# A last layer of 2304 tokens: its first product by a seven-product scheme in three blocks of 768 tokens

## The chip, the cores and the metric

The kernel runs on one core of a Trainium2 chip. The metric is the device time of one execution in microseconds (us); the time before is the median of three runs. The trace is of one profiled execution. Engines: PE is TensorE, ACT is ScalarE, DVE is VectorE, POOL is GpSimd, SP issues the transfers.

## What is computed

The reference chains three layers: linear attention, a top-2 mixture of eight experts, and a last dense layer over all 2304 tokens of 512 features. The change concerns the last layer, and the gather that feeds it:

```python
out[mask] += top2_w[mask, k, None] * (h @ w2[e])   # experts, two per token
...
h = np.maximum(x @ w_in, 0.0)                      # 2304x512 @ 512x2048
return (h * h @ w_out).astype(np.float32)          # 2304x2048 @ 2048x512
```

## The kernel before

**Order.** The scheduling is manual: each engine runs its instructions in the order in which the Python code emits them, and semaphores join the engines. So the loops of the code are the order of the work. SP issues transfers in order too, and so does POOL with its gathers.

**Exact products from split numbers.** Every fp32 matrix is split in two fp32r parts, `hi` (a rounded copy, by ACT) and `lo` (the rest, a subtraction). A product takes three matmuls: hi·hi, hi·lo, lo·hi (`mm`, L97). Weights are loaded in pieces of 128x512 (`w_load`, L131) and split by ACT and POOL (`w_conv`, L136).

**Experts.** Ten parts (`for pt in range(1, NP)`, L1161), each of eight steps `f`. A step has the first product of its tokens (`e_1`) and the second one of the step before (`e_2`, L240). The last part, 9, has 352 tokens of expert 7. Each expert writes its rows to `y_d` in DRAM. Beside parts 2 to 8 the last layer's weights are widened into `win_d` and `wout_d`.

**Last layer.** Tokens come in 18 tiles of 128. `l_gather` (L1022) issues two indirect transfers on POOL for a tile, the rows `ya` and `yb` of its two experts; `l_sum` (L1038) weighs and adds them on ACT and DVE; `l_t` (L1044) transposes on PE and splits. There are five blocks, four of 512 tokens and one of 256. In a block, for each of 16 slices of 128 hidden features, `l_1` (L1057) makes 12 matmuls into a PSUM bank M0 or M1, ACT takes the relu and the rounded square, DVE the exact square and the low part; `l_2` (L1076) adds the slice's second product to one accumulator per token tile, one slice later:

```python
for u in range(NU + 1):
    m, f = divmod(u, NF2)
    if u < NU:
        l_1(u)
    if u > 0:
        l_2(u - 1)
```

The weights of the layer stay split in SBUF for all blocks; half of their pieces are loaded and split in parts 8 and 9, half in block 0. The four tiles of block 0 are gathered in part 9. They may read only rows of `y_d` that earlier parts have written (`YA_ROWS`); the router (`r_4`, L694) adds to a count when this would not do, and a slow path (L1222) then recomputes everything.

Of the kernel before, what the change touches and what calls it, by code (L numbers as in the profile page):

```python
# [32 lines left out]
def kernel(  # L33
# [25 lines left out]
    NTILE = B * R + B // 2  # L59
    DC = DM // 128  # L60
# [48 lines left out]
    runs = consts.tile([128, E], FT)  # L109

# [145 lines left out]
    with ExitStack() as actx:  # L256
# [437 lines left out]
        def r_4(g):  # L694
# [4 lines left out]
            yield  # L699
            nc.vector.tensor_add(runs, t[:, 1, 0], runs)  # L700
# [32 lines left out]
        def r_6(g):  # L733
# [211 lines left out]
    nc.vector.tensor_reduce(cf, runs, axis=AX.X, op=OP.max)  # L945
    nc.vector.tensor_copy(ci, cf)
# [7 lines left out]
    with ExitStack() as ectx:  # L954
# [63 lines left out]
        blocks = [[T0[b] + r for r in range(R)] for b in range(B)]  # L1018
        blocks.insert(1, [T0[b] + R for b in (1, 3)])
        X2, H2, OP_, YA = {}, {}, {}, {}  # L1020

        def l_gather(m, i):  # L1022
            t = blocks[m][i]
            if m == 0:
                if i == 0:
                    YA[-1] = ep.tile([128, R, DM], FT, name="ya0", tag="xg", bufs=1)
                ya = YA[-1][:, i]
                yb = ep.tile([128, DM], FT, name="yb", tag="wide", bufs=3)
            else:
                ya = ep.tile([128, DM], FT, name="ya", tag="ya", bufs=3)  # L1030
                yb = ep.tile([128, DM], FT, name="yb", tag="wide", bufs=3)
# [12 lines left out]
        def l_t(m, i):  # L1044
            ya, _ = YA.pop((m, i))
            if i == 0:
                X2[m] = [ep.tile([128, DC, 512], FR, name="x2", tag=x, bufs=1)
                         for x in (("xth", "xtl") if m % 2 == 0 else ("xg", "wd"))]
            t = bank("Tk" if m else ("Tk", "N0", "KV", "M0")[i], [128, DC, 128])
            for d in range(DC):  # L1050
                nc.tensor.transpose(t[:, d], ya[:, d * 128:d * 128 + 128], ident)  # L1051
            c = slice(i * 128, i * 128 + 128)
            hi_lo(X2[m][0][:, :, c], X2[m][1][:, :, c], t)

        NF2 = F2 // 128

        def l_1(u):  # L1057
            m, f = divmod(u, NF2)
            n = 128 * len(blocks[m])
            wh, wl = wt[2 * E + f // 4, 0]  # L1060
            fc = (f % 4) * 128
            xh, xl = X2[m]
            t = bank(f"M{u % 2}", [128, 512])
            for d in range(DC):
                for i, (a, b) in enumerate(((wh, xh), (wh, xl), (wl, xh))):
                    mm(t[:, :n], a[:, d, fc:fc + 128], b[:, d, :n], d == 0 and i == 0, d == DC - 1 and i == 2)
            r = ep.tile([128, 512], FT, name="r", tag="y", bufs=4)
            nc.scalar.activation(r[:, :n], t[:, :n], AF.Relu)  # L1068
            hh = ep.tile([128, 512], FR, name="h2h", tag="hh", bufs=2)
            hl = ep.tile([128, 512], FR, name="h2l", tag="hl", bufs=2)  # L1070
            nc.scalar.activation(hh[:, :n], r[:, :n], AF.Square)  # L1071
            nc.vector.tensor_mul(r[:, :n], t[:, :n], r[:, :n])  # L1072
            nc.vector.tensor_sub(hl[:, :n], r[:, :n], hh[:, :n].bitcast(FT))  # L1073
            H2[u] = (hh, hl)

        def l_2(u):  # L1076
            m, f = divmod(u, NF2)
            wh, wl = wt[2 * E + f // 4, 1]
            hh, hl = H2.pop(u)
            last = f == NF2 - 1  # L1080
            for j, tt in enumerate(blocks[m]):
                if f == 0:
                    OP_[j] = bank(ACC[j], [128, DM])
                c = slice(j * 128, j * 128 + 128)
                for i, (a, b) in enumerate(((hh, wh), (hh, wl), (hl, wh))):
                    mm(OP_[j], a[:, c], b[:, f % 4], f == 0 and i == 0, last and i == 2)
# [25 lines left out]
        for f in range(NF2 // 2):  # L1112
            pieces[NP, f], ahead = ahead[:2], ahead[2:]
# [212 lines left out]
```

## Time and profile before

| | us |
|---|---|
| median of 3 runs (lowest, highest) | 1069.35 (1068.01, 1069.85) |
| the profiled execution's own time | 1067.83 |
| its span in the trace | 1066.0 |
| PE busy | 1038.9 (97%) |
| DVE, ACT, POOL busy | 595.0, 471.1, 396.7 |

The span is what the trace covers; the execution's own time is 1.8 us longer. Busy time of matmuls is of overlapping instructions, so the rate of a stretch is better read from the chain of waits, which gives the start and the length of runs of instructions.

### The profile page before, as it was taken

Reading aid. Unit: us, or ns where it says so; the run is one execution under the profiler, and the core shown is the slowest. Engines: PE = TensorE matmul, PEld = TensorE weight load, DVE = VectorE, ACT = ScalarE, POOL = GpSimd, SP = SyncE. Lnnn points to the kernel's source line nnn. Section 1 sums busy time; section 2 is a strip of 40 time slices with the busy share of each in tenths; the row PEclk is TensorE's granted clock in tenths of the full one; section 3 lists DMA queues with packets and bytes.
Section 4 is the critical chain, followed back from the end, with each engine's and each line's share of the span. In section 5 each row is a group of like instructions: output and inputs, shape, how many; then the busy total and the mean of one; then the engine's idle time right before and its main releaser. Section 6 shows DMA issues by size and latency. Waiting matters only on the chain.

```text
span 1066.0 us, 18597 instructions
## 1 busy us (share of the span) xinstructions
PE 1038.9 (97%) x7132; PEld 874.8 (82%) x7132; DVE 595.0 (56%) x1192; ACT 471.1 (44%) x967; POOL 396.7 (37%) x374
## 2 busy tenths in 40 slices
PE   6999999899999999999999999999999999999997
PEld 4777677888888898998888888888988888888886
DVE  5778798812777777777778743432442332333222
ACT  4887777335354444535353544432332222222221
POOL 3444656645546454645545455540110010000000
PEclk9999999999999999999999999999999999999999
DMA  5976633465646465565656554320220011001001
GB/s 149 280 213 212 191 115 121 149 199 188 203 156 201 163 196 192 196 204 167 205 183 208 161 174 130 114 79 5 65 70 13 28 40 40 21 0 40 1 1 42
DMA packets 104048, 136.27 MB, mean 128 GB/s; under 512 B 17554, under 2 KB 58642, under 8 KB 103954
## 3 DMA queue, kind: packets, MB, share of 16 engines
q1 hardware_dynamic: 98194, 116.14, 34.8%
q0 software_dynamic: 5760, 18.88, 5.4%
q8 instruction: 58, 0.95, 0.4%
q14 instruction: 36, 0.29, 0.1%
HBM read 92.45 MB, written 42.54 MB: 127 GB/s over the span
## 4 chain that ended last, share of the span: by engine, by line
PE 90%; DVE 6%; ACT 2%; DMA 1%; issue 1%; POOL 0%; SPq 0%; ACTq 0%
PE M L98 38%; PE N L98 15%; PE KV L98 12%; PE Tq L98 8%; PE P L98 8%; PE kpair L98 2%; PE qpair L98 1%; DVE kd L428 1%; DVE kmx L426 1%; PE Tk L393 1%; PE M L200 1%; PE Tk L98 1%; PE Tk L1051 1%; PE Tk L200 1%; PE Tk L403 1%; DVE ps L513 1%
## 5 line engine op out<-in xcount | busy, mean ns | idle before, releaser
L1072 DVE TENSOR_TENSOR r<-M,r 128x512 f32<-128x512 f32 (+1 forms) x80 | 51.0, 638 | 248.3 <-ACT h2h L1071 248.3
L1068 ACT ACTIVATE r<-M 128x512 f32<-128x512 f32 (+1 forms) x80 | 44.5, 556 | 250.7 <-PE M L98 250.7
L229 ACT ACTIVATE hh<-M 128x304 fp32r<-128x304 f32 (+2 forms) x128 | 49.0, 422 | 210.6 <-PE M L98 210.3
L226 DVE SCALAR_TENSOR_TENSOR hl<-M,hh 128x304 fp32r<-128x304 f32 (+2 forms) x128 | 56.2, 470 | 109.1 <-ACT hh L229 109.0
L508 POOL PARTITION_ALL_REDUCE qmx<-ps x36 | 69.9, 1944 | 79.6 <-ACT ps L506 67.2
L1033 POOL DMA_INDIRECT ya<-y_d,yrows x18 | 17.9, 997 | 189.3 <-PE Tk L1051 113.6
L1073 DVE TENSOR_TENSOR h2l<-r,h2h 128x512 fp32r<-128x512 f32 (+1 forms) x80 | 57.7, 722 | 7.0
L1071 ACT ACTIVATE h2h<-r 128x512 fp32r<-128x512 f32 (+1 forms) x80 | 47.1, 589 | 2.5
L98 PE MATMUL M<-x,w30h 128*128 128x512 f32 (+1 forms) x160 | 46.1, 373 | 0.0
L98 PE MATMUL M<-x,w10h 128*128 128x512 f32 (+1 forms) x160 | 45.9, 372 | 0.0
L98 PE MATMUL M<-x,w20h 128*128 128x512 f32 (+1 forms) x160 | 45.8, 371 | 0.0
L98 PE MATMUL M<-x,w00h 128*128 128x512 f32 (+1 forms) x160 | 45.6, 369 | 0.0
L145 POOL TENSOR_TENSOR w30l<-wstage,w30h 128x512 fp32r<-128x512 f32 x20 | 27.7, 1386 | 46.7 <-ACT w30h L144 46.6
L98 PE MATMUL N<-kvc,qp 128*64 128x81 f32 x1024 | 42.6, 236 | 1.7 <-DVE runs L700 1.1
L145 POOL TENSOR_TENSOR w20l<-wstage,w20h 128x512 fp32r<-128x512 f32 x20 | 27.9, 1395 | 43.1 <-ACT w20h L144 29.4
L98 PEld LDWEIGHTS N<-kvc,qp 128*64 128x64 f32 x1024 | 37.8, 137 | 5.7 <-issue 4.4
L769 POOL DMA_INDIRECT xg_d<-x,slots x32 | 32.9, 1030 | 12.2 <-issue 5.6
L145 POOL TENSOR_TENSOR w10l<-wstage,w10h 128x512 fp32r<-128x512 f32 x16 | 22.9, 1434 | 38.2 <-ACT w10h L144 35.1
L1003 POOL TENSOR_TENSOR wx<-wx 128x256 f32<-128x256 f32 x32 | 23.6, 737 | 34.4 <-DVE wx L999 34.1
L1003 POOL TENSOR_TENSOR wd<-wd 128x256 f32<-128x256 f32 x32 | 23.5, 735 | 34.6 <-DVE wd L999 34.6
L98 PE MATMUL KV<-kp,vt 128*64 128x256 f32 x256 | 35.1, 395 | 0.0
L1008 DVE SCALAR_TENSOR_TENSOR wd<-wd 128x256 f32<-128x256 f32 x32 | 34.1, 1067 | 1.1
(432 smaller groups left out, 3258.2 us busy)
## 6 DMA issues: line engine op xcount, KB each, us to landing
wstage<-in_moe_w_dram SPq DMA_DIRECT2D x128, 256.0 KB, 3.8
xg_d<-zero SPq DMA_DIRECT2D x8, 1216.0 KB, 7.7
y_d<-y SPq DMA_DIRECT2D x32, 256.0 KB, 2.2
wide<-in_moe_w_in_dram SPq DMA_DIRECT2D x32, 256.0 KB, 3.5
wide<-in_moe_w_out_dram SPq DMA_DIRECT2D x32, 256.0 KB, 3.0
xg<-xg_d SPq DMA_DIRECT2D x7, 1024.0 KB, 6.4
kt<-in_k_dram SPq DMA_DIRECT2D x16, 256.0 KB, 4.0
vt<-in_v_dram SPq DMA_DIRECT2D x16, 256.0 KB, 3.8
```

The source lines that it names most:

```text
L98: nc.tensor.matmul(o, l, r, start=start, stop=stop, skip_group_check=True)
L145: (nc.gpsimd if n >= 2 else nc.vector).tensor_sub(lo[:, c], src, hi[:, c].bitcast(FT))
L226: nc.vector.scalar_tensor_tensor(hl[:, c0:c1], o, 0.0, hh[:, c0:c1].bitcast(FT), op0=OP.max, op1=OP.subtract)
L229: nc.scalar.activation(hh[:, c[1]:c[2]], c[0], AF.Relu)
L508: nc.gpsimd.partition_all_reduce(mx, ps, 128, bass.bass_isa.ReduceOp.absmax)
L769: st = nc.gpsimd.indirect_dma_start(out=xg_d, out_offset=bass.IndirectOffsetOnAxis(ap=slots[:, T0[g] + i, c:c + 1], axis=0), in_=src, in_o ...
L1003: nc.gpsimd.tensor_mul(part, part, exp)
L1008: nc.vector.scalar_tensor_tensor(exp, ok, TINY * TINY, exp, op0=OP.is_ge, op1=OP.mult)
L1068: nc.scalar.activation(r[:, :n], t[:, :n], AF.Relu)
L1071: nc.scalar.activation(hh[:, :n], r[:, :n], AF.Square)
L1072: nc.vector.tensor_mul(r[:, :n], t[:, :n], r[:, :n])
L1073: nc.vector.tensor_sub(hl[:, :n], r[:, :n], hh[:, :n].bitcast(FT))
```

## The change

In place of `l_1` and `l_2` by slices there are three blocks of 768 tokens (six tiles), each of eight sets. A set `u` has 256 hidden features. Its first product, 256 features by 768 tokens over 512 inputs, is cut in 2x2 blocks of 128 features by 256 inputs and 256 inputs by 384 tokens, and made from seven products (`product`) in place of eight, each of six matmuls of 128x384. Two PSUM banks hold the running sums (`b0`, `b1`, banks M0 and M1); ACT copies (`snap`) and DVE additions (`plus`) combine them to the four quarters `c11`, `c12`, `c21`, `c22`. The operands are sums of weight blocks (`a_sums` on DVE, split by `a_conv` on ACT and POOL, once per set, one set ahead) and of token blocks (`x_sum` on DVE, split by `x_conv` on ACT and DVE, seven operands once per block, in the last set of the block before and the first of its own). `l_h` makes the squares, `l_2` the second product of a quarter. The weights of a set are loaded anew in every block (`a_load`, `o_load`, `o_conv`). The six tiles of block 0 are gathered, added and transposed inside part 9.

```diff
+            for c, rows in ((slice(0, n), YA_ROWS), (slice(n, G), NS)):
...
+        def x_conv(m, i):
+            t = wpa.tile([128, 2, 2, LH], FR, name="xo", tag=("w00h", "w00l", "w01h", "w01l", "w10h", "w10l", "w11h")[i])
+            x = x_op(m, i)
+            nc.scalar.activation(t[:, 0], x, AF.Copy)
+            nc.vector.tensor_sub(t[:, 1], x, t[:, 0].bitcast(FT))
...
+            nc.vector.tensor_add(s[:, 0], a21, a22)
+            nc.vector.tensor_sub(s[:, 2], a11, a21)
+            nc.vector.tensor_sub(s[:, 1], s[:, 0], a11)
+            nc.vector.tensor_sub(s[:, 3], a12, s[:, 1])
...
+                nc.scalar.activation(h[:, c], x, AF.Copy)
+                nc.gpsimd.tensor_sub(l[:, c], x, h[:, c].bitcast(FT))
...
+            nc.scalar.activation(q[:, 0], c, AF.Square)
+            nc.vector.tensor_mul(c, c, c)
+            nc.vector.tensor_sub(q[:, 1], c, q[:, 0].bitcast(FT))
...
+            product(u, 1, b0, True)
+            s1 = snap(b0, "hh")
+            product(u, 2, b1, True)
+            c11 = plus(b1, s1)
+            if u:
+                for f in range(2):
+                    o_conv(u, f)
+            gap(1, 1)
+            l_h(u, 0, 0, c11)
+            ops(end, (x_conv, 0))
+            ops(begin, (x_sum, 5))
+            if u + 1 < NU:
+                a_sums(u + 1)
+            product(u, 6, b0, False)
+            u2 = snap(b0, "hl")
+            product(u, 5, b1, True)
+            s5 = snap(b1, "hh")
+            ops(begin, (x_conv, 5), (x_conv, 2))
+            if due:
+                l_sum(nxt * LB + s - 1)
+            ops(end, (x_conv, 1), (x_conv, 4))
+            if u + 1 < NU:
+                a_conv(u + 1)
+            gap(0, 1)
+            product(u, 7, b0, False)
+            c22 = plus(b0, s5)
+            ops(end, (x_conv, 3))
+            ops(begin, (x_conv, 6))
+            gap(1, 0)
+            l_h(u, 1, 1, c22)
+            product(u, 3, b1, False)
+            c12 = plus(b1, u2)
+            product(u, 4, b0, False)
+            c21 = relu(b0)
+            l_h(u, 0, 1, c12)
+            l_h(u, 1, 0, c21, True)
...
+            l_2(u, 0, 0, (lambda: l_t(nxt * LB + s - 1, "M1")) if due else None)
...
+                if s == NSET - 2:
+                    x_sum(nxt, 3)
+                    x_sum(nxt, 4)
+                if s == NSET - 1:
+                    x_sum(nxt, 6)
...
-        ahead = [(n, i, c) for n in range(2, 2 * E + 4) for c in range(4) for i in range(2)]
-        per = [0] + [2 * NF] * (NP - 3) + [NF, NF]
+        ahead = [(n, i, c) for n in range(2, 2 * E) for c in range(4) for i in range(2)]
+        per = [0] + [2 * NF] * (NP - 3) + [0, 0]
...
-        for i in range(R):
-            l_t(0, i)
-        e_2(NP - 1, NF - 1)
```

`gap(f, half)` is `l_2` of that quarter of the set before. `begin` is true in the first set of a block (set 0), `end` in its last (set 7).

**PE, one ordinary set.** `xo` and `wa` are the operands of the seven products, `hq` and `wo` those of the second product, `ident` marks a transposition. Before, a slice has 12 rows of `l_1` and 12 of `l_2`; at the seam of the two stands:

```order
L98 MATMUL M_8303<-x_8049,w10h 128x512
L98 MATMUL M_8303<-x_8050,w10h 128x512
L98 MATMUL M_8303<-x_8049,w10l 128x512
L98 MATMUL N_8149<-w11h,h2h 128x512
L98 MATMUL N_8149<-w11l,h2h 128x512
L98 MATMUL N_8149<-w11h,h2l 128x512
```

Now a set, up to its fifth product:

```order
L101 MATMUL M_8357<-xo,wa 128x384 x6
L101 MATMUL M_8358<-xo,wa 128x384 x6
L101 MATMUL P<-wo,hq 128x512 x3
L101 MATMUL Tq<-wo,hq 128x512 x3
L101 MATMUL N_8237<-wo,hq 128x512 x3
L101 MATMUL M_8357<-xo,wa 128x384 x6
L101 MATMUL M_8358<-xo,wa 128x384 x6
L101 MATMUL P<-wo,hq 128x512 x3
L101 MATMUL Tq<-wo,hq 128x512 x3
L101 MATMUL N_8237<-wo,hq 128x512 x3
L101 MATMUL M_8357<-xo,wa 128x384 x6
L101 MATMUL N_8189<-wo,hq 128x512 x3
```

Products 1, 2, 6, 5, 7, 3, 4 stand in this order; nine matmuls of the second product stand behind products 2, 5, 7 and 4. The four products on b0 (1, 6, 7, 4) use one bank, the three on b1 the other, so each must wait until ACT or DVE has read that bank.

**DVE, set 7 of a block.** Rows L1135 are `plus`, L1153 and L1154 the squares, L1087 to L1090 the weight sums, L1065 token sums, L1071 low parts of token operands. Before, DVE had two rows per slice:

```order
L1072 TENSOR_TENSOR r<-M_10200,r 128x512
L1073 TENSOR_TENSOR h2l<-r,h2h 128x512
L1072 TENSOR_TENSOR r<-M_10236,r 128x512
L1073 TENSOR_TENSOR h2l<-r,h2h 128x512
L1042 SCALAR_TENSOR_TENSOR ya<-yb,gates,ya 128x512
```

Now, from the end of set 6 to `c22` of set 7:

```order
L1065 TENSOR_TENSOR xs<-xr,xs 128x768
L1135 TENSOR_TENSOR c<-M_9082,snap 128x384
L1153 TENSOR_TENSOR c<-c 128x384
L1154 TENSOR_TENSOR hq<-c,hq 128x384
L1071 TENSOR_TENSOR xo<-xr,xo 128x768
L1087 TENSOR_TENSOR wr<-wr 128x256
L1088 TENSOR_TENSOR wr<-wr 128x256
L1089 TENSOR_TENSOR wr<-wr 128x256
L1090 TENSOR_TENSOR wr<-wr 128x256
L1071 TENSOR_TENSOR xo<-xr,xo 128x768
L1071 TENSOR_TENSOR xo<-xs,xo 128x768
L1135 TENSOR_TENSOR c<-M_9081,snap 128x384
```

The additions that empty a bank (`plus`) now stand behind token and weight operands in DVE's queue.

**POOL, last layer.** L145 are the low parts of weight pieces, L1033 (now L1032) gathers, L1115 and L1099 the low parts of a set's weights. Before, in block 0:

```order
L145 TENSOR_TENSOR w31l<-wstage,w31h 128x512
L1033 DMA ya<-y_d,yrows 128x512
L1033 DMA yb<-y_d,yrows 128x512
L145 TENSOR_TENSOR w30l<-wstage,w30h 128x512
L145 TENSOR_TENSOR w31l<-wstage,w31h 128x512
L1033 DMA ya<-y_d,yrows 128x512
```

Now a set has this:

```order
L1115 TENSOR_TENSOR wo<-wo 128x512 x2
L1099 TENSOR_TENSOR wa<-wr,wa 128x512
L1099 TENSOR_TENSOR wa<-wr,wa 128x256
L1099 TENSOR_TENSOR wa<-wr,wa 128x1024
L1032 DMA ya<-y_d,yrows 128x512
L1032 DMA yb<-y_d,yrows 128x512
```

Before, POOL had gathers alone from block 1 on; now five subtractions of weight parts stand in every set, and gathers in six sets each of blocks 0 and 1.

## Rows read from the trace of the kernel before

**Rows 1.** The page's chain that ended last, shares by engine.
```profile
PE 90%; DVE 6%; ACT 2%; DMA 1%; issue 1%; POOL 0%; SPq 0%; ACTq 0%
```
**Rows 2.** Stretches: length, busy of PE, PEld, DVE, ACT, POOL (instructions), PEclk, DMA share, GB/s.
```profile
647.24:1059.42 412.18, 411.48 (x1926) 341.67 (x1925) 137.20 (x202) 127.52 (x223) 52.69 (x46) 1.00 0.13 39
664.00:720.00 56.00, 56.00 (x250) 46.01 (x249) 22.58 (x24) 21.20 (x36) 29.89 (x24) 1.00 0.35 99
```
**Rows 3.** The chain of waits in time: start, us, what; part 9, blocks 0, 1, 2 and 4.
```profile
647.24 1.92 PE M L98 x12
...
651.23 0.44 PE Tk L1051 x4
...
746.38 1.43 PE M L98 x12
...
790.45 2.73 PE M L98 x12
...
1051.12 2.75 PE M L98 x12
...
1056.60 0.70 PE N L98 x3
...
1058.00 0.69 PE P L98 x3
1058.70 0.70 PE Tq L98 x3
1059.42 0.69 DVE o L1090
```
**Rows 4.** Instructions in time, first slice of block 0: start, us, what, idle before and releaser.
```profile
659.84 1.28 POOL L145 TENSOR_TENSOR w20l<-wstage,w20h 128x512 fp32r<-128x512 f32 x1 [8.29 <-ACT w20h L144]
659.94 1.73 DVE L1073 TENSOR_TENSOR h2l<-r,h2h 128x512 fp32r<-128x512 f32 x1
...
661.08 1.74 POOL L145 TENSOR_TENSOR w21l<-wstage,w21h 128x512 fp32r<-128x512 f32 x1
...
661.72 0.50 PE L98 MATMUL N<-w01h,h2l 128*128 128x512 f32 x1 [0.67 <-DVE h2l L1073]
```
**Rows 5.** The same view of DVE and POOL in an expert part.
```profile
378.25 1.29 POOL L145 TENSOR_TENSOR w01l<-wstage,w01h 128x512 fp32r<-128x512 f32 x1
379.25 0.86 DVE L226 SCALAR_TENSOR_TENSOR hl<-M,hh 128x304 fp32r<-128x304 f32 x2 [2.11 <-ACT hh L229]
...
380.20 1.29 POOL L145 TENSOR_TENSOR w00l<-wstage,w00h 128x512 fp32r<-128x512 f32 x1
380.27 1.50 DVE L1007 TENSOR_TENSOR wd<-wd 128x256 f32<-128x256 f32 x1 [0.17 <-POOL wd L1003]
381.45 1.46 POOL L145 TENSOR_TENSOR w01l<-wstage,w01h 128x512 fp32r<-128x512 f32 x1
```
**Rows 6.** Groups of DVE by line and form: busy us, mean ns, idle before.
```profile
L102 DVE TENSOR_TENSOR xtl<-M,xth 128x384 fp32r<-128x384 f32 x8 | 4.5, 557 | 1.5 <-ACT xth L101 1.3
L1072 DVE TENSOR_TENSOR r<-M,r 128x512 f32<-128x512 f32 x64 | 44.3, 692 | 224.3 <-ACT h2h L1071 224.3
L1073 DVE TENSOR_TENSOR h2l<-r,h2h 128x256 fp32r<-128x256 f32 x16 | 6.8, 425 | 1.3
```
**Rows 7.** The same view of ACT.
```profile
L101 ACT ACTIVATE xth<-M 128x384 fp32r<-128x384 f32 x8 | 3.9, 490 | 3.0 <-PE M L200 3.0
L1071 ACT ACTIVATE h2h<-r 128x512 fp32r<-128x512 f32 x64 | 40.4, 632 | 2.0
L1071 ACT ACTIVATE h2h<-r 128x256 fp32r<-128x256 f32 x16 | 6.7, 417 | 0.5
```
**Rows 8.** The same view of POOL.
```profile
L1003 POOL TENSOR_TENSOR wd<-wd 128x256 f32<-128x256 f32 x32 | 23.5, 735 | 34.6 <-DVE wd L999 34.6
```
**Rows 9.** Transfers issued from 619 to 700 us: KB each, median us to landing.
```profile
wstage<-win_d SPq DMA_DIRECT2D x11, 256.0 KB, 3.5
...
ya<-y_d,yrows POOLq DMA_INDIRECT x6, 3.7
```

More of the change, by code (lines that the diff above doesn't have):

```diff
@@ L59 @@
     NTILE = B * R + B // 2
+    LB = 6
+    NB = NTILE // LB
+    LH = LB // 2 * 128
     DC = DM // 128
@@ L1015 @@
         last_in, last_out = (win_d, wout_d) if wide else (w_in, w_out)
[L1018 to L1031, printed above, removed]
+        YA, XR, XS, XO, WR, LW, WO, WB, HQ, OP_ = {}, {}, {}, {}, {}, {}, {}, {}, {}, {}
@@ L1055 @@
[L1055 to L1074, printed above, removed]
@@ new lines, with product, snap @@
+        PAIRING = {1: (0, 0), 2: (1, 1), 3: (6, 2), 4: (2, 6), 5: (3, 3), 6: (4, 4), 7: (5, 5)}
+        def product(u, p, o, start):
+            a, b = PAIRING[p]
+            h, l = LW[u]
+            x = XO[u // NSET, b]
+            for c in range(2):
+                for i, (w, k) in enumerate(((h, 0), (h, 1), (l, 0))):
+                    mm(o, w[:, a, c], x[:, k, c], start and c == 0 and i == 0, c == 1 and i == 2)
+        def snap(o, tag):
+            t = ep.tile([128, LH], FT, name="snap", tag=tag, bufs=2)
+            nc.scalar.activation(t, o, AF.Copy)
+            return t
@@ L1084, in l_2 @@
+        def l_2(u, f, half, within=None):
+            m, s = divmod(u, NSET)
+            q, w = HQ.pop((u, f, half)), WO[u, f]
+            first, last = s == 0 and f == half, s == NSET - 1 and f != half
+            for j in range(LB // 2):
+                n = half * (LB // 2) + j
+                if first:
+                    OP_[n] = bank(ACC6[n], [128, DM])
                 c = slice(j * 128, j * 128 + 128)
-                for i, (a, b) in enumerate(((hh, wh), (hh, wl), (hl, wh))):
-                    mm(OP_[j], a[:, c], b[:, f % 4], f == 0 and i == 0, last and i == 2)
+                for i, (a, b) in enumerate(((0, 0), (0, 1), (1, 0))):
+                    mm(OP_[n], q[:, a, c], w[:, b], first and i == 0, last and i == 2)
+                if within and j == 1:
+                    within()
@@ L1111 @@
                 pieces[pt, f], ahead = ahead[:n], ahead[n:]
-        for f in range(NF2 // 2):
-            pieces[NP, f], ahead = ahead[:2], ahead[2:]
         assert not ahead
-        order = [(pt, f) for pt in range(1, NP) for f in range(NF)] + [(NP, f) for f in range(NF2)]
+        order = [(pt, f) for pt in range(1, NP) for f in range(NF)]
         todo = [p for o in order for p in pieces.get(o, [])]
@@ L1222 @@
+        assert not wide or (WF[0] == NW and not WP and not WS)
+        j0, j1 = parts[NP - 1][1:]
+        for u in range(NU):
+            l_set(u, [lambda j=j: e_2(NP - 1, NF - 1, [j]) for j in range(j0, j1)])
+        l_2(NU - 1, 1, 1)
+        l_2(NU - 1, 0, 1)
+        l_2(NU - 1, 1, 0)
     with tc.If(most > CAP):
```

232 lines of the change are left out of this document (166 added, 66 removed).

## The prediction

> **What bounds the kernel now.** I read the views from coarse to fine. The chain that ended last gives PE 90% of the span [rows 1]. [...] So a matmul less is time less, and every new wait of PE is time more. [...] The one wait is in the timeline of the first slice: PE waits 0.67 us for a DVE subtraction, which took 1.73 us because POOL was subtracting when it began [rows 4]. That wait is the key to the rest.
>
> **What PE saves.** Before, the first product is 64 groups of 12 matmuls of 512 columns, 2.73 or 2.75 us a group, and 16 groups of 256 columns at 1.43 us [rows 3]: 64 x 2.74 + 16 x 1.43 = 198.2 us. The change makes 24 sets x 42 = 1008 matmuls of 384 columns, which the trace doesn't have. By the nearest rows, 352 columns cost 1.92 / 12 = 0.160 us and 512 cost 2.74 / 12 = 0.228, so 384 lie between those ends, near the first: 0.174 on the line through both. A product of six is 1.04 us, all of them 175.1. Saved: 23.1 us. The second product keeps its columns, nine matmuls at 2.07 us behind a product [rows 3], and 18 transpositions at 0.44 us stay 18 (six instead of four now in part 9). The old wait of 0.67 goes too. PE gains 23.8 us if nothing new makes it wait.
>
> **The price of the new side work.** ACT: 384 columns cost 0.49 us from PSUM; from SBUF the line through 0.417 (256) and 0.632 (512) gives 0.52, for 768 0.85, for 1024 1.06 [rows 7]. DVE: 0.557 for 384; 0.425 and 0.692 for 256 and 512 [rows 6], so 0.96 for 768. POOL: 1.29 for 512 and 0.735 for 256 [rows 5, 8], so 2.40 for 1024. The loads come to 1 MB per set of 15.6 us, 67 GB/s, where 99 ran beside a PE that never waited [rows 2]; they are issued a set ahead and land in about 3.5 us, a gather in 3.7 [rows 9]. Gathers and weight sums stay hidden. In part 9 the six gathers follow the last stores they need; their tiles come two or three steps of 4 us later. The weight pieces taken out of parts 8 and 9 free engines that PE didn't wait for: nothing. The router's lines are a few tiny DVE instructions: nothing, at most 0.3 us. The end is the same copy and store behind the last matmul: nothing.
>
> **The rule that decides.** The timeline shows that POOL and DVE take turns. A DVE subtraction of two SBUF tensors that begins during a POOL subtraction ends only after it, 1.73 for 0.69 us [rows 4, 6] and 1.50 for about 0.42 [rows 5, 6], and the POOL one behind it waits in turn, 1.74 for 1.29. A DVE instruction with one input in PSUM isn't held: two of them take 0.86 us in the middle of a POOL subtraction [rows 5]. [...] I go by the turns.
>
> **An ordinary set** takes PE 7 x 1.04 + 4 x 2.07 = 15.6 us, 16.0 with a transposition. At the port POOL needs 2.58 + 1.29 + 0.74 + 2.40 = 7.0 and DVE 8 x 0.557 + 4 x 0.425 + 0.7 = 6.9 us, 13.9 together: it fits. Walked in queue order from product 1 (time 0), c11 is there at 2.7, the last POOL part of the next set's weights at 12.8, c12 at 14.5, 2.5 us before its bank is wanted, and DVE ends 1.9 us into the next set. No wait.
>
> **A block boundary** adds ten DVE instructions of 768 columns to two sets: three in-place sums and seven low parts, less two gather sums. The port then needs 37 us in two sets that last 31. Walked from product 1 of set 7: token sums 3 and 4 with a POOL turn between them hold c11 until 5.6, so product 5 waits 0.45. The low part of operand 0, four weight sums, operand 1, a POOL turn and operand 4 stand before c22: 14.3, and product 4 waits 1.4. c12 comes at 19.5, behind a turn of 2.4, and product 2 of the new block waits 1.1. There c11 stands behind four square instructions, a sum and two turns: 26.9, or 25.6 if one turn falls the other way, and product 5 waits 3.3 or 2.0. From c11 runs a chain of relu, square, two DVE instructions, sum 5, four weight sums and the low part of operand 5: product 7 waits 2.6. Operand 6 comes behind the 1024-column turn: product 4 waits 2.2. Sum 10.9 or 9.6, I take 10.3; two boundaries, 20.6. Ends: 1.2 a boundary if there were no turns, 14 if POOL's parts cost 15% more.
>
> **The start** is a boundary without held-back second products to fill it. By the same walk product 7 of the first set waits 4.4 us for operand 5, products 3 and 4 wait 1.2 and 0.7, the next set's product 5 about 1.0: 7.3 (5 without turns).
>
> **Sum.** -23.8 + 20.6 + 7.3 = +4.1 us: a span of 1070.1 and an own time of 1067.83 + 4.1 = 1071.9. The median of the runs is 1.5 us above the profiled execution, so I predict 1069.35 + 4.1 = 1073.5. What a measurement can tell from no change is about 0.2%, 2.1 us.
>
> **Rivals.** (a) The forecast, with waits of 20 to 34 us in all: -4 to +10, its own range 1066 to 1079. Chance 0.55: slower 0.38, same 0.12, faster 0.05. (b) The operands made ahead are hidden as the change says: turns cost little when POOL's queue has run dry, only the chain to operand 5 shows. Waits 2 x 1.2 + 5, so -16.4: 1053. For it: outside the boundary every bank is read 2.5 us early. Against: rows 4. It decides if c11 of set 0 comes before 23 us of the walk. Chance 0.18, faster. (c) Half of that: c11 is in time, products 7 and 4 wait, 4.8 a boundary: 9.6 + 7.3 - 23.8 = -6.9, 1062.5. Chance 0.12 (faster 0.08, same 0.04). (d) Slower still: POOL's parts cost more than the line, the ordinary sets slip too. It begins when a set's POOL and DVE turns exceed 16 us, 15% on both; half a us on each of 21 sets adds 10: 1084. Chance 0.15. That the change falls into the slow path is excluded: the reference's own routing sends 206 rows of the first six tiles to expert 7, under the limit of 256, and no expert more than 597 rows under 608. The granted clock stayed at 1.00 through all of part 9 and the last layer; a wait of 3 us might drop it, which no row here prices.
>
> So faster 0.31, same 0.16, slower 0.53. The range leaves out part of (b) and the tail of (d): 1055 to 1081.
>
> **What would show it.** Right: 1008 matmuls of 384 columns at 0.174 us; ordinary sets of 15.6 to 16.0 us with no PE wait; waits of PE at sets 0, 8 and 16 and at the ends of sets 7 and 15, released by DVE lines 1071 and 1135; DVE subtractions of 768 columns stretched by POOL. Wrong: PE solid through the boundaries (b), or gaps in every set (d). A granted clock below 1.00 inside the sets would break the price of every matmul.

## The result and the profile after

| | before | after |
|---|---|---|
| median of five runs each (lowest, highest), us | 1068.42 (1068.01, 1069.85) | 1075.74 (1075.41, 1079.24) |
| ratio, 95% interval | | 1.0073 [1.0056, 1.0091] |
| span of the profiled execution, us | 1066.0 | 1073.8 |
| mean granted clock over the span | 0.998 | 0.992 |

Slower by 0.7%, three to four times what this measurement can tell from no change. The prediction was 1073.5, slower as the likeliest sign. The kernel after is called the changed kernel below.

The page of the changed kernel (busy time by engine; shares of the chain that ended last; groups of instructions with busy us, mean ns, idle before):

```profile
PE 1029.2 (96%) x7180; PEld 888.9 (83%) x7180; DVE 729.5 (68%) x1408; ACT 575.2 (54%) x1180; POOL 532.6 (50%) x462
...
PE 80%; DVE 12%; ACT 4%; issue 2%; DMA 2%; SPq 0%; ACTq 0%; DVEq 0%
...
L101 PE MATMUL M<-xo,wa 128*128 128x384 f32 x1008 | 197.8, 342 | 13.4 <-DVE c L1135 4.5
...
L1153 DVE TENSOR_TENSOR c<-c 128x384 f32<-128x384 f32 x96 | 87.5, 911 | 89.6 <-ACT hq L1152 89.6
...
L1135 DVE TENSOR_TENSOR c<-M,snap 128x384 f32<-128x384 f32 x72 | 39.7, 552 | 39.5 <-PE M L101 28.1
...
L1154 DVE TENSOR_TENSOR hq<-c,hq 128x384 fp32r<-128x384 f32 x96 | 57.5, 599 | 3.4
```

PE is busy 9.7 us less than before, and the span is 7.8 us longer. In the chain, against [rows 1], PE falls from 90% to 80% and DVE doubles from 6% to 12%: the chain now runs through DVE at the waits. Line 1153, the exact square, takes 0.911 us on average; [rows 6] give 0.557 for 384 columns. That group alone shows how often DVE stood behind POOL. Line 1135, `plus`, has one input in PSUM and as many columns: all 72 of them take 0.54 to 0.56 us, though 41 ran wholly inside a POOL subtraction.

All waits of PE from 600 us to the end (engine, tile, line; releaser; sum, count, longest):

```profile
PE M L101 <- DVE c L1135: 4.5, 2, 2.3
PE M L101 <- ACT xo L1070: 3.8, 3, 2.5
PE M L101 <- DVE xo L1071: 3.0, 3, 1.0
PE KV L1049 <- DVE ya L1040: 2.4, 1, 2.4
PE M L101 <- ACT c L1140: 1.7, 2, 1.0
PE N L1049 <- DVE ya L1040: 0.6, 1, 0.6
PE Tk L101 <- ACT o L1178: 0.5, 1, 0.5
PE Tk L1049 <- DVE ya L1040: 0.5, 1, 0.5
```

Before, PE stood still for 0.7 us from the last expert step on [rows 2]; here it is 17 us. Three places have them: the transpositions of part 9 (L1049), the first set of block 0, and the first sets of blocks 1 and 2. L1135 and L1071 are the releasers that the forecast named; the waits at L1049, and those for ACT's output copy and relu of c21 (L1178, L1140), it didn't name at all.

Stretches of the changed kernel, columns as in [rows 2]:

```profile
652.00:656.00 4.00, 2.84 (x13) 2.67 (x14) 1.64 (x3) 1.69 (x3) 0.00 (x0) 0.68 0.00 0
672.00:676.00 4.00, 4.00 (x17) 3.73 (x17) 3.79 (x4) 1.54 (x3) 3.85 (x3) 0.76 0.03 6
804.00:808.00 4.00, 4.00 (x14) 3.34 (x13) 4.00 (x5) 1.54 (x4) 4.00 (x3) 0.62 0.36 136
940.00:944.00 4.00, 3.84 (x11) 3.42 (x12) 4.00 (x6) 2.38 (x4) 4.00 (x3) 0.57 0.11 42
```

At each of these places, behind the waits, the granted clock falls to 0.50 for 3.4 us: means of 0.57 to 0.76 over the stretches. Before it was 1.00 throughout [rows 2]. In the stretches at 804 and 940 us DVE and POOL are busy all the time.

Where the 7.8 us came from, by the starts of parts and sets in PE's timeline (the time from one set's first matmul to the next one's):

| term of the sum | predicted | measured | from |
|---|---|---|---|
| PE saves | -23.8 | -21.5 | sets without waits 15.70 and 16.14 |
| two boundaries | +20.6 | +16.4 | first sets 24.36 and 23.27, second sets 0.1 over |
| start | +7.3 | +5.9 | first set 17.36, 11.5 without waits |
| part 9 | 0 | +5.6 | 39.5 us, 33.9 without waits |
| ahead of part 9, and the end | 0 | +1.5 | 0.4 and 1.1 |
| sum | +4.1 | +7.9 | span +7.8 |

Part 9 without waits is worked out from the kernel before: 35.1 us, less nine matmuls that now stand in set 0 (2.1), and two tiles more to transpose (0.9). "Without waits" is also without the lower clock: in each measured loss a part is waits and the rest is matmuls at the lower clock and the restart behind a wait (behind the wait of 2.26 us below, six matmuls take 1.32 us; the six before it take 1.22). PE stood still for 3.4 of the 5.6 us in part 9, for 3.6 of the 5.9 at the start, and for 10.3 of the 16.4 at the boundaries.

Here is how a boundary looks in time, DVE, POOL and PE of the changed kernel (start, us, what, idle before and releaser; set 0 of block 1 begins at 789.59):

```profile
784.87 4.53 POOL L1099 TENSOR_TENSOR wa<-wr,wa 128x256 fp32r<-128x256 f32 x2
787.35 2.47 DVE L1153 TENSOR_TENSOR c<-c 128x384 f32<-128x384 f32 x1 [0.21 <-ACT hq L1152]
...
793.38 2.95 POOL L1115 TENSOR_TENSOR wo<-wo 128x512 fp32r<-128x512 f32 x2 [3.98 <-ACT wo L1114]
793.68 1.53 DVE L1154 TENSOR_TENSOR hq<-c,hq 128x384 fp32r<-128x384 f32 x1
795.13 2.01 DVE L1065 TENSOR_TENSOR xs<-xr,xs 128x768 f32<-128x768 f32 x1
797.07 0.55 DVE L1135 TENSOR_TENSOR c<-M,snap 128x384 f32<-128x384 f32 x1
797.67 1.32 PE L101 MATMUL M<-xo,wa 128*128 128x384 f32 x6 [2.26 <-DVE c L1135]
802.17 0.95 DVE L1071 TENSOR_TENSOR xo<-xs,xo 128x768 fp32r<-128x768 f32 x1
803.17 1.59 PE L101 MATMUL M<-xo,wa 128*128 128x384 f32 x5 [1.01 <-DVE xo L1071]
804.55 1.49 PE L101 MATMUL N<-wo,hq 128*128 128x512 f32 x3
```

This is the walk of the forecast: a square of 0.56 us held to 2.47 by the 1024-column piece, later a square and a token sum held by two pieces of the second product's weights, and c11 (797.07), which needs no turn itself, queued behind them. PE's product 5 waits 2.26, product 7 1.64 in two pieces (0.63 for the high part of operand 5, 1.01 for the low one). The last row is three matmuls of the second product at the lower clock: 1.49 us, where 0.86 is usual.

### The profile page after: what moved, and what is told of

Read it like the earlier page. It is cut to its first block, busy times and chain, and to the rows that moved or that the text cites. A ratio compares the mean times of both kernels' runs of the same rounds, so it can differ in the third digit from the quotient of the medians.

```text
span 1073.8 us, 19254 instructions
## 1 busy us (share of the span) xinstructions
PE 1029.2 (96%) x7180; PEld 888.9 (83%) x7180; DVE 729.5 (68%) x1408; ACT 575.2 (54%) x1180; POOL 532.6 (50%) x462
## 4 chain that ended last, share of the span: by engine, by line
PE 80%; DVE 12%; ACT 4%; issue 2%; DMA 2%; SPq 0%; ACTq 0%; DVEq 0%
PE M L101 33%; PE N L101 15%; PE KV L101 10%; PE Tq L101 7%; PE P L101 7%; PE Tk L101 3%; DVE xo L1071 2%; PE kpair L101 2%; DVE c L1153 1%; DVE kd L432 1%; DVE kmx L430 1%; PE qpair L101 1%; DMA out_dram<-o 1%; PE M L204 1%; DVE xs L1065 1%
## 5 line engine op out<-in xcount | busy, mean ns | idle before, releaser
L101 PE MATMUL M<-xo,wa 128*128 128x384 f32 x1008 | 197.8, 342 | 13.4 <-DVE c L1135 4.5
L101 PEld LDWEIGHTS M<-xo,wa 128*128 128x128 f32 x1008 | 181.0, 190 | 26.1 <-DVE c L1135 6.1
L1099 POOL TENSOR_TENSOR wa<-wr,wa 128x512 fp32r<-128x512 f32 (+2 forms) x72 | 113.3, 1598 | 93.9 <-ACT wa L1098 93.9
L1153 DVE TENSOR_TENSOR c<-c 128x384 f32<-128x384 f32 x96 | 87.5, 911 | 89.6 <-ACT hq L1152 89.6
L230 DVE SCALAR_TENSOR_TENSOR hl<-M,hh 128x304 fp32r<-128x304 f32 (+2 forms) x128 | 56.2, 470 | 116.8 <-ACT hh L233 116.8
L1115 POOL TENSOR_TENSOR wo<-wo 128x512 fp32r<-128x512 f32 x48 | 64.7, 1369 | 103.1 <-ACT wo L1114 103.1
L101 PE MATMUL N<-wo,hq 128*128 128x512 f32 x288 | 83.3, 398 | 0.0
L1135 DVE TENSOR_TENSOR c<-M,snap 128x384 f32<-128x384 f32 x72 | 39.7, 552 | 39.5 <-PE M L101 28.1
L1130 ACT ACTIVATE snap<-M 128x384 f32<-128x384 f32 x72 | 35.0, 488 | 52.1 <-PE M L101 51.9
L101 PEld LDWEIGHTS N<-wo,hq 128*128 128x128 f32 x288 | 54.4, 191 | 8.4
L1154 DVE TENSOR_TENSOR hq<-c,hq 128x384 fp32r<-128x384 f32 x96 | 57.5, 599 | 3.4
L1152 ACT ACTIVATE hq<-c 128x384 fp32r<-128x384 f32 x96 | 47.8, 521 | 2.3
L1098 ACT ACTIVATE wa<-wr 128x512 fp32r<-128x512 f32 (+2 forms) x72 | 45.4, 691 | 5.1 <-DVE wr L1090 5.1
```

The costliest lines, as they stand in the source:

```text
L101: nc.tensor.matmul(o, l, r, start=start, stop=stop, skip_group_check=True)
L230: nc.vector.scalar_tensor_tensor(hl[:, c0:c1], o, 0.0, hh[:, c0:c1].bitcast(FT), op0=OP.max, op1=OP.subtract)
L1098: nc.scalar.activation(h[:, c], x, AF.Copy)
L1099: nc.gpsimd.tensor_sub(l[:, c], x, h[:, c].bitcast(FT))
L1115: nc.gpsimd.tensor_sub(t[:, 1], r, t[:, 0].bitcast(FT))
L1135: nc.vector.tensor_add(c, o, t)
```

## The experiments

Two theories on the cause were tested first, T1 and T2. T1: POOL's subtractions hold DVE's two-input ones, turn by turn, and so delay the chains PE waits for. T2: DVE's own work and its order in the queue are the cause, whatever POOL does. Where the prediction and the expectations speak of a port, the rows show the turns alone, 1.73 us for 0.69 [rows 4, 6]; that a port lies behind them was not shown. Two more came with the traces. T3: the stretches at the lower clock come from PE's waits and cost some 1.7 us each (an estimate, half of 3.4 at 0.50). T4: output copies and quarters wait for stores. The six experiments from "The low parts of the weights on DVE" to "The wait filled" ran on chips where the kernel before takes 1078.4 to 1078.9 us; their mean granted clock over the span is 0.985 to 0.991, and in "Both" and "The wait filled" stretches of 4 us between 200 and 240 us, ahead of the change, have means of 0.50 to 0.90. So they are read by their ratio to the kernel before, and by their parts from part 9 on. Where a ratio is turned into us, it is times 1068.4.

### Without POOL's low parts

```diff
-                nc.gpsimd.tensor_sub(l[:, c], x, h[:, c].bitcast(FT))
-            LW[u] = (h, l)
+            LW[u] = (h, h)
...
-            nc.gpsimd.tensor_sub(t[:, 1], r, t[:, 0].bitcast(FT))
...
-                    mm(OP_[n], q[:, a, c], w[:, b], first and i == 0, last and i == 2)
+                    mm(OP_[n], q[:, a, c], w[:, 0], first and i == 0, last and i == 2)
```

> Leaves out the low parts of the last layer's weights: POOL's subtractions for a_conv and o_conv are gone, and the matmuls that read a low part read the high part instead, so PE's work is unchanged. Theory T1 (POOL and DVE take turns at the shared port, and POOL's turns delay the DVE chains): the first sets of blocks 1 and 2, which lasted 24.4 and 23.3 us, come to 17 to 19 us; expert step 7 of part 9 starts about 4 us earlier; the start loses 4.5 to 5 of its 5.8 us still. In all 1058 to 1063 us. Theory T2 (DVE's own amount and order of work is the cause, turns hardly matter): those sets stay above 22 us, 1071 to 1075 us.

Measured: 1060.18 us, ratio 0.9927 [0.9910, 0.9943], 15.6 us below the changed kernel with the same work of PE. The first sets of blocks 1 and 2 last 17.5 and 17.6 us in place of 24.4 and 23.3, part 9 takes 34.9 in place of 39.5. The start alone stays: 18.1 us, with waits of 3.5 us, as in the changed kernel (3.6). The waits of PE from 600 us on:

```profile
PE M L101 <- ACT xo L1070: 2.5, 1, 2.5
PE M L101 <- ACT c L1138: 1.7, 2, 1.3
PE M L101 <- DVE xo L1071: 1.0, 1, 1.0
...
PE Tk L1049 <- DVE ya L1040: 0.5, 1, 0.5
```

Every wait for c11 is gone, as is the 2.4 us one of the transpositions. What is left is the start's chain to operand 5 and the output copies. POOL's share of the boundaries and of part 9 is shown; it has none in the start.

### Without new token operands

```diff
         def x_sum(m, i):
+            if m:
+                return
...
         def x_conv(m, i):
+            if m:
+                return
...
-            x = XO[u // NSET, b]
+            x = XO[0, b]
```

> Leaves out the token operands of blocks 1 and 2: their sums and splits are not made, and the products read the operands of block 0. All else stays: gathers, transposes, weight sums, output copies and stores. If the operands are the whole of the boundary's loss, the first sets of blocks 1 and 2 take 15.7 to 16.0 us and the time is 1058.5 to 1060.5 us. If the output copies that wait for stores (theory T4) have a loss of their own there, 1 to 1.7 us stay in or just behind each of them: 1061 to 1063 us.

Measured: 1062.52 us (1060.11 to 1066.20, seven runs), ratio 0.9949 [0.9934, 0.9964]. The first set of block 2 is 15.70 us, that of block 1 18.34: it has one wait of 2.5 us for the relu of c21, whose ACT instruction waited for a store of the output to free its buffer. That is a wait as T4 expects it, in one boundary of two. So block 2's boundary closes when the token operands go, block 1's but for that wait (13.2 us in all), and both nearly close when POOL's parts go (15.6 us, part 9 among them): it takes both to make them late.

### Operand 0 one step later in part 9

```diff
                     if f == 5:
-                        x_conv(0, 0)
...
                     if f == 6:
+                        x_conv(0, 0)
                         x_conv(0, 1)
```

> In part 9 the split of operand 0 is issued one expert step later, behind the additions and transposes of the last tiles, beside operand 1. If the 5.4 us lost in part 9 come from that one DVE subtraction in front of the token additions, expert step 7 starts near 650.3 us in place of 654.5 and the half-clock stretch behind it is gone: 1070.0 to 1071.7 us. If the additions wait for gathers or for ACT instead, or the start loses what part 9 gains, since the operands come no earlier: less than 1.5 us gained, 1074 to 1076 us.

Measured: 1076.83 us, ratio 1.0079: a miss. The waits in part 9 fell from 3.4 to 2.4 us only, and the start grew from 17.4 to 19.2 us, waiting for operands that now came later. In the changed kernel I had read the operand's subtraction as the cause, held from 647.75 for 4.13 us. Without it the token addition itself is held. The first three rows are of the changed kernel:

```profile
643.71 4.88 POOL L1099 TENSOR_TENSOR wa<-wr,wa 128x512 fp32r<-128x512 f32 x3
647.75 4.13 DVE L1071 TENSOR_TENSOR xo<-xr,xo 128x768 fp32r<-128x768 f32 x1 [1.68 <-ACT xo L1070]
648.55 2.51 POOL L1115 TENSOR_TENSOR wo<-wo 128x512 fp32r<-128x512 f32 x2
```

And these of the experiment:

```profile
649.09 2.52 POOL L1115 TENSOR_TENSOR wo<-wo 128x512 fp32r<-128x512 f32 x2
649.21 2.95 DVE L1040 SCALAR_TENSOR_TENSOR ya<-yb,gates,ya 128x512 f32<-128x512 f32 x1 [2.60 <-ACT ya L1039]
```

In both, DVE's instruction ends only after both pieces of L1115. It isn't one turn each: these two instructions of DVE, which met a run of POOL instructions, were held through three and two of them.

### Output copies in a ring of their own

```diff
-            y = ep.tile([128, DM], FT, name="o", tag="y", bufs=4)
+            y = ep.tile([128, DM], FT, name="o", tag="ya" if n > 2 else "wide", bufs=3)
```

> The output copies use the six buffers of the gathered rows (3 and 3) in place of the four that the quarters c11 to c22 share. Theory T4 (copies and quarters wait for stores): the wait of the last copy at the end goes, 1.05 us, and the one behind product 4 in the first sets of blocks 1 and 2, 0.5 to 1.7 us each: 1072 to 1074 us. If the stores are hidden behind the DVE chain anyway, only the end gains: 1074.3 to 1075 us. The gathers of the next block use the same buffers later than the stores land, so they cost nothing.

Measured: 1075.25 us, ratio 1.0075 [1.0056, 1.0094]: no gain that can be told. The waits behind product 4 are gone, and first sets shrink to 22.4 us, but in block 1 the second set grows from 16.25 to 19.01 us with two waits for DVE (L1135, 1.2 each). At the end the last copy no longer waits for a store, yet the time from PE's last matmul to the span's end stays 7.6 us. T4 falls as a cause of its own: the stores only stand in front of a backlog of DVE that PE meets a little later.

### The low parts of the weights on DVE

```diff
-                nc.gpsimd.tensor_sub(l[:, c], x, h[:, c].bitcast(FT))
+                nc.vector.tensor_sub(l[:, c], x, h[:, c].bitcast(FT))
...
-            nc.gpsimd.tensor_sub(t[:, 1], r, t[:, 0].bitcast(FT))
+            nc.vector.tensor_sub(t[:, 1], r, t[:, 0].bitcast(FT))
```

> The low parts of the last layer's weights are made by DVE in place of POOL; nothing is left out. DVE gets some 3.9 us more per set (0.69, 0.43 and about 1.4 us in place of POOL's 1.38, 0.92, 2.49), POOL has only gathers left. Theory T1 (a POOL turn costs the port more than the same subtraction on DVE, and no turns are left to wait through): the first sets of blocks 1 and 2 lose 3 to 5 us each in place of 8.7 and 7.6, part 9 loses under 1.5: 1062 to 1067 us. Theory T2 (DVE's own amount of work is the bound at the boundaries): some 8 us more in each boundary: 1082 us or more.

Measured: ratio 0.9992 [0.9982, 1.0002], equal to the kernel before and 8.7 us below the changed kernel on its scale. Two groups of DVE by form:

```profile
L1153 DVE TENSOR_TENSOR c<-c 128x384 f32<-128x384 f32 x96 | 53.4, 556 | 65.1 <-ACT hq L1152 65.1
...
L1099 DVE TENSOR_TENSOR wa<-wr,wa 128x1024 fp32r<-128x1024 f32 x24 | 29.4, 1225 | 2.6 <-ACT wa L1098 1.3 <-issue 0.2
```

The square is back at 0.556 us, and the 1024-column part takes 1.225 us where POOL took 2.485 in the changed kernel, 2.03 times as long, turns included:

```profile
L1099 POOL TENSOR_TENSOR wa<-wr,wa 128x1024 fp32r<-128x1024 f32 x24 | 59.6, 2485 | 2.6 <-ACT wa L1098 2.6
```

DVE was given 87 us of new work and the boundaries became shorter: first sets of 20.5 and 20.4 us. T2 alone, which expected 8 us more in each, falls. But 4.8 and 4.7 us of the first sets stay, with no POOL turn to blame, and the time, 1067.5 us by its ratio, is just above T1's range. So T1 isn't the whole cause.

### The square on ACT

```diff
-            nc.vector.tensor_mul(c, c, c)
+            nc.scalar.activation(c, c, AF.Square)
```

> The exact square is taken by ACT in place instead of DVE's product; nothing is left out, four DVE instructions a set less, four ACT ones of about 0.5 us more. T1 and T2 both expect the boundaries to shrink: each instruction taken from DVE gives back its 0.56 us and, by T1, the POOL turn it waits through (0.91 measured on average): losses of 3 to 5 us in place of 8.7 and 7.6, part 9 and the start as they are: 1066 to 1070 us; T2 alone (0.56 each, 4.5 a boundary at most): 1068 to 1072 us. A rival: the chain relu, square, square on ACT becomes the late one and the time stays at 1074 us or above.

Measured: ratio 1.0051 [1.0034, 1.0068], 2.4 us below the changed kernel, less than either theory expected. The first sets fall by 3.3 us each, to 21.1 and 20.0, but the ordinary sets of blocks 0 and 1 rise from 16.14 to 16.40: ACT becomes late in them. Half of the gain is given back there.

### Part 9 and the start, first try

```diff
                     if f == 6:
                         x_conv(0, 1)
+                        for x in range(2):
+                            o_conv(0, x)
...
                         x_sum(0, 6)
+                        x_sum(0, 5)
+                        x_conv(0, 5)
+                        x_conv(0, 2)
```

> Two edits at places apart in time. In part 9 the split of the second weights of set 0 moves one expert step later, behind the last token additions: T1 (the addition was held through POOL's run of instructions) expects the waits before expert step 7 to fall from 3.4 us to under 1 and its half-clock stretch to go. The start makes operands 5, 2 and 6 of block 0 ahead of set 0: the first set, 17.4 us, comes to 12 to 13.5 us. Both: 1066 to 1069 us. Rival: the port is full there too, the earlier work only moves the waits to products 3 and 4 and to set 1: 1072 to 1075 us.

Measured: ratio 1.0109, worse. The first edit works: the wait of 2.4 us for the transposition is gone. The second lengthens the first set from 17.4 to 25.3 us. Its waits:

```profile
PE M L101 <- ACT snap L1130: 2.9, 1, 2.9
PE M L101 <- DVE xo L1071: 2.8, 1, 2.8
PE M L101 <- DVE hl L230: 1.7, 1, 1.7
```

Operands made early stand in DVE's and ACT's queues ahead of the low part of the last expert step (L230) and of the copy that frees the bank (L1130). This speaks for T2: what is put in front of a short, urgent instruction in an in-order queue is paid at once.

### The squares behind c11

```diff
-            l_h(u, 0, 0, c11)
+            if LATE:
+                LATE.pop(0)()
+                x_sum(m, 6)
+                own = l_h(u, 0, 0, c11, defer=True)
+                x_sum(m, 5)
+                LATE.pop(0)()
+                x_conv(m, 5)
+                own()
```

> At the two block boundaries the DVE squares of the last two quarters and sum 6 stand behind c11 of the new block in place of ahead of it, and sum 5 and operand 5 ahead of the weight sums. T2 (order in DVE's queue is the cause): the 2.3 us wait for c11 and the waits for operand 5 go, 6 to 10 us in all: 1066 to 1070 us. T1 (the port is full for two sets, whatever the order): the wait for c11 goes, but more than half of it comes back behind later products (operand 6, c21 or the next set): 1071 to 1074.5 us.

Measured: ratio 1.0086 [1.0069, 1.0103], 1.4 us above the changed kernel; neither theory's range. The wait of 2.3 us for c11 goes, but other products now wait, mostly for low parts of operands (L1071, seven waits, 7.2 us in all with the start's), and the first sets last 24.6 and 23.9 us. Taken alone, this looked like T1, turns that fill the time whatever the order; the last two runs show that it was a poor order.

### Both: weights on DVE and a new order

The start was done otherwise than in the first try (weight sums and high parts of set 1 and token sum 5 in part 9, operands 5 and 2 ahead of the squares of c11), and the first sets of blocks 1 and 2 were put in order of need.

```diff
-            l_h(u, 0, 0, c11)
+            if first:
+                if u:
+                    x_sum(m, 5)
+                    l_h(u, 0, 0, c11)
+                x_conv(m, 5)
...
-            ops(begin, (x_conv, 5), (x_conv, 2))
+            if first:
+                x_conv(m, 2)
+                if u:
+                    a_sums(u + 1)
+                    a_high(u + 1)
```

> Nothing is left out. The low parts of the weights are on DVE as in weights_on_dve, the output copies in the six buffers of the gathered rows as in own_ring, and the order is new at three places. Start: the weight sums and high parts of set 1 and token sum 5 are made in part 9, operands 5 and 2 stand ahead of the squares of c11. First sets of blocks 1 and 2: sum 5 and operand 5 ahead of the weight sums and the second product's weights, the weights' low parts behind c22 and operand 6, the output copies 3 to 5 on ACT. By T1 (less port time, then order pays): first sets of about 13 us at the start (17.8 before the reordering) and 16 to 18 us at the boundaries (20.5): 1057 to 1061 us on a chip where the kernel before takes 1068, a ratio of 0.990 to 0.994. By T2's opposite, that reordering only moves the waits: 0.998 or above.

Measured: ratio 0.9977 [0.9967, 0.9987], outside T1's range. The start is right, 13.7 us. The boundaries are not: 21.4 and 21.0 us, with this row as the largest:

```profile
PE N L101 <- DVE wo L1130: 3.8, 2, 1.9
```

The second product's weights of the same set had been put behind the next set's weights, and came 1.9 us too late in both.

### The wait filled

```diff
+            if begin is not None and u:
+                for _ in range(12):
+                    mm(OP_[0][:, :LH], XO[m, "zero"], XO[m, 1][:, 0, 0], False, False)
             product(u, 6, b0, False)
```

> The changed kernel with twelve added matmuls of 384 columns by a stationary of zeros in each of the first sets of blocks 1 and 2, placed where PE waits 2.3 us for c11; they add zero to a running sum and fill that wait, nothing else changes but one small ACT instruction per block. Theory T3 (the half-clock stretches come from PE standing still, and cost of their own): the stretches at about 804 to 807 and 940 to 944 us go, and 1.5 to 1.8 us each: the first sets of blocks 1 and 2 last 22.6 and 21.6 us in place of 24.4 and 23.3. Rival (the clock falls for another reason): they stay, and the sets are as long as in the changed kernel or longer.

Measured: ratio 1.0066 [1.0048, 1.0084], no different from the changed kernel. PE's wait for c11 shrank to 0.2 us in both blocks. In block 1 the stretch at the lower clock stayed; in block 2 it went. Two stretches of this kernel, columns as above, one in either block:

```profile
816.00:818.00 2.00, 2.00 (x6) 1.56 (x5) 2.00 (x5) 0.49 (x1) 2.00 (x2) 0.50 0.15 59
952.00:956.00 4.00, 3.83 (x19) 3.43 (x20) 4.00 (x6) 2.39 (x4) 4.00 (x3) 1.00 0.10 39
```

In block 2, at the full clock (1.00), a wait of 1.3 us for operand 6 took the place of the slow matmuls, and the set was 0.5 us shorter (22.8), not 1.7. So T3 falls as far as this one block shows: at a boundary DVE sets the pace, and a slow PE only arrives later at the next wait. Why the clock stayed low in block 1 is open, and part 9 and the start weren't tried apart.

### The order mended, and the same order with POOL

```diff
                 x_conv(m, 2)
                 if u:
-                    a_sums(u + 1)
-                    a_high(u + 1)
+                    x_conv(m, 6)
+                    for f in range(2):
+                        o_conv(u, f)
+                    a_high(u + 1, slice(0, 2))
...
+                if u:
+                    a_sums(u + 1)
+                a_low(u + 1)
             l_h(u, 1, 1, c22)
...
             c21 = relu(b0)
+            if first:
+                a_high(u + 1, slice(2, 3))
+                a_low(u + 1)
```

> As best1, nothing left out, but in the first sets of blocks 1 and 2 operand 6 and the second product's weights stand ahead of c22, the output copies and the weight sums, and the last of the three weight pieces of the next set behind c21, at the start too. In best1 PE waited there 1.3 us for operand 5 and 1.9 us for the second product's weights, and a half-clock stretch followed. By T1 (DVE alone now needs about 16.5 us in a set of 15.7 us, so order decides): first sets of 16 to 17.5 us and second sets of 16.1 to 16.6 us at the boundaries in place of 21.4 and 17.2, the set behind the start 16.2 in place of 16.9; a ratio to the kernel before of 0.986 to 0.991. If a new wait takes their place: 0.995 or above.

Measured: 1053.01 us (1052.48 to 1053.73), ratio 0.9857 [0.9841, 0.9873]: 1.4% faster than the kernel before and 2.1% faster than the changed one. All of PE's waits from 600 us to the end:

```profile
PE M L101 <- DVE xo L1071: 0.5, 1, 0.5
PE Tk L1049 <- DVE ya L1040: 0.5, 1, 0.5
PE KV L1049 <- DVE ya L1040: 0.4, 1, 0.4
PE N L1049 <- DVE ya L1040: 0.4, 1, 0.4
PE M L101 <- DVE c L1153: 0.2, 1, 0.2
```

The list has no wait at the boundaries: the first sets last 15.71 us each, at the full clock (1.00). The second set of block 1 is 0.5 us longer than without waits (16.64) and the sets 7 are 0.2, in pauses too short for the list. The last run puts only the subtractions back on POOL:

```diff
-                AL[u].append(lambda c=c, x=x: nc.vector.tensor_sub(l[:, c], x, h[:, c].bitcast(FT)))
+                AL[u].append(lambda c=c, x=x: nc.gpsimd.tensor_sub(l[:, c], x, h[:, c].bitcast(FT)))
...
-            nc.vector.tensor_sub(t[:, 1], r, t[:, 0].bitcast(FT))
+            nc.gpsimd.tensor_sub(t[:, 1], r, t[:, 0].bitcast(FT))
```

> best2 with one thing undone: the low parts of the weights are POOL's again; order, buffers and copies as in best2. Theory T1 (the POOL turns are the larger half; order pays only once the port has room): the first sets of blocks 1 and 2 last 19 to 23 us in place of 15.7, part 9 loses 2 to 4 us, 1065 to 1072 us on a chip where the kernel before takes 1068, a ratio of 0.997 to 1.004. Theory T2 (order is the cause, who subtracts hardly matters): 15.7 to 17 us for those sets, 1053 to 1057 us, 0.986 to 0.990.

Measured: 1065.07 us, ratio 0.9962 [0.9948, 0.9976], just under T1's range and far above T2's. The first sets last 16.6 us, shorter than T1 expected, and the delay sits in the second ones, 18.5 and 20.4 us:

```profile
PE M L101 <- DVE c L1153: 4.1, 7, 2.1
PE KV L1049 <- DVE ya L1040: 2.3, 1, 2.3
PE M L1049 <- DVE c L1153: 1.5, 2, 1.0
```

The four kernels by place (us; a boundary is its sets 7, 0 and 1, 47.1 or 47.5 without waits; part 9 from its first matmul to set 0):

| | part 9 | start, sets 0 and 1 | boundary 1 | boundary 2 | ratio to before |
|---|---|---|---|---|---|
| changed kernel | 39.5 | 33.5 | 56.3 | 54.8 | 1.0073 |
| weights on DVE alone | 36.0 | 34.0 | 54.2 | 52.1 | 0.9992 |
| new order alone, weights on POOL | 39.5 | 30.9 | 50.8 | 52.7 | 0.9962 |
| both | 36.1 | 29.8 | 48.3 | 47.3 | 0.9857 |

Against the changed kernel the places add up to 7.8 us less for the engine alone, 10.2 for the order alone, 22.6 for both. In these four kernels part 9 moves with the engine alone; but the first try at part 9 shows that order can do as much there, 35.6 us with POOL's subtractions in place. The start is mostly the order's: 2.6 of 3.7 us. The boundaries need both: 4.8 there for the engine, 7.6 for the order, 15.5 together. Without the turns DVE has time for an order in which almost nothing is late; with them no order tried here did that. That order was made for DVE doing the subtractions, and one made for POOL wasn't tried. The row "new order alone" contains the ring and ACT copies of the output too; they weren't taken apart from it.

## Why the prediction was right, and where it was not

**Sign and size.** Right: the time lies within the range, 2.2 us above the number given. Its case (a) happened in its time, not in its waits: PE stood still for 17 us, against 20 to 34, and the lower clock, which was in no term, made up for much of it. That the number came so close is partly luck: by the table the terms missed by 9.4 us one way (PE's saving, part 9, the ends) and by 5.6 the other (boundaries, start).

**What PE saves.** The mechanism was right and the size 2.3 us too large. A product lasts 1.05 us, not 1.04, nine matmuls 2.09, not 2.07, so the sets without waits take 15.70 and 16.14, where the prices add up to 15.56 and 16.00: 3.4 us over 24 sets. Against it stands that the first product of the kernel before took 199.7 us by the starts of its matmuls, not 198.2. The remaining 0.4 us I can't place.

**Ordinary sets.** Right: no wait of PE in any of the sets 2 to 6, and the work of POOL, DVE and the queues fits with room.

**The boundary.** Right in mechanism for two of its waits, 16.4 for 20.6 us in all. The first sets lost 8.7 and 7.6 us where some 8.5 were walked, but that agreement is luck: PE stood still for only 5.6 and 4.8 us of it, and most of the rest is the stretch at the lower clock, which the walk had at nothing. As walked came product 5 (2.3 us for 3.3 or 2.0: c11 behind four squares, a sum and turns) and, shorter, product 7 (1.6 for 2.6: the chain to operand 5). Product 2 waited 0.1 us for 1.1, and product 4 not at all for operand 6 (2.2); the waits for ACT's output copy and relu (1.5 and 0.7 us) were not in the walk. The step that failed whole is set 7: 1.85 us predicted, none measured (15.70). There c11 was done 3.7 us into the set, not 5.6, and c22 12.3 us into it, not 14.3: fewer turns fell in front of them than the walk had put there. Two slips in the sums are small: the six waits add up to 11.05 or 9.75 us, not 10.9 or 9.6, and the need of POOL and DVE, 27.8 for two sets and 9.6 for ten instructions less 1.4 for two gather sums, is 36 us, not 37.

**The start.** Right in place, 5.9 for 7.3. But only product 7 waits, 3.6 us for 4.4; the other three waits didn't come, and the lower clock took their place. Nor are the turns its cause, to which the prediction gave 2.3 of its 7.3 us: without POOL's subtractions the waits are the same and the set is no shorter (18.1).

**"Gathers and weight sums stay hidden", part 9 at nothing.** Wrong by 5.6 us, and the largest error. The tiles came in time; what was late were the additions, behind POOL's split of the first set's weights, which the prediction hadn't walked in that part. Without POOL's subtractions 4.6 of the 5.6 us go. The walk was made for boundaries and start alone.

**The end at nothing.** Wrong by 1.1 us. Seven stores stand at the end where four stood; a freed buffer didn't help, so I count it to the stores, which no run took apart.

**The clock.** The prediction said that no row priced a drop. The one drop of the kernel before stands behind its last matmul: PE is still from 1059.4 us and the clock is at 0.50 from 1061.7. In the changed kernel it did drop inside the work, to 0.50 for 3.4 us at four places, behind waits of PE with 2.3 to 2.5 us as the longest, and the one stretch that the filled wait removed gave back 0.5 us of its 1.7: there it was mostly hidden behind DVE's backlog.

**The rivals.** (b), the operands hidden, was given 1053. It was to decide by c11 of set 0 coming before 23 us of the walk; it came at 23.7. The mended kernel reaches just that time, 1053.0: the saving of PE was there, and the change's order and choice of engine lost it. If POOL and DVE shared one rate in place of taking turns, the boundaries would have lost what the need exceeds, 12 us (37 less 31 at each; 10 with a need of 36), an estimate from the prediction's own numbers, where the turns gave 20.6; the 16.4 measured lie between and don't tell the two apart. The rows do: a square of 0.56 us held to 2.47 and a subtraction of 0.95 to 4.13 are more than half the rate would make of them. The row by which the prediction had PSUM inputs free of turns was thin, since its two instructions began 0.3 us before POOL's ended; the 41 instructions of L1135 that ran inside a POOL subtraction, at 0.54 to 0.56 us, bear it out.

## What to carry to other kernels

When one engine's work is cut close to the bound, look at how the side work meets in time, not at its busy share: DVE was at 68%, and ten instructions more in two sets at each boundary, with the start, cost 22.3 us, more than the 21.5 that were saved. Before giving a subtraction to an idle POOL, count what DVE's two-input instructions lose behind it, here 0.911 us for a square of 0.556; DVE doing both was faster in these runs. And in an in-order queue, sort by when each result is wanted: the reads that free a bank first, the operands of this set next, those of the next set last.

## What the runs showed of the hardware

- A two-input DVE instruction that met a run of POOL subtractions was held through more than one of them: 4.13 us for 0.95, through the rest of a 1024-column piece and two of 512; 2.95 us for 0.75 (its price with the weights on DVE) through two.
- Without POOL's subtractions DVE had its plain price again: the square 0.911 us with them, 0.556 without.
- The granted clock fell to 0.50 for 3.4 us at four places of the changed kernel, behind PE's waits of 2.4 us in part 9, of 2.5 and 1.0 at the start, and of 2.3, 0.6 and 1.0 at both boundaries. With the wait filled, the waits there were 0.2, 0.6 and 1.0 us in both blocks: the clock fell to 0.50 behind them in block 1 and stayed at 1.00 in block 2.
